# The gate's row sums on VectorE instead of TensorE, in a gated mix of local attention and a token MLP

## The chip, the cores and the metric

The kernel runs on one core of a Trainium2 chip. The metric is the device time of one execution in microseconds (us), as a median of several runs; lower is better. The core has a matmul engine (TensorE, PE in the profile; its weight loads are PEld), a vector engine (VectorE, DVE), a scalar engine for activations (ScalarE, ACT), and GpSimd (POOL). SyncE (SP) issues most DMA transfers; ACT issues some. Each engine works through its own list of instructions in order, and semaphores hold an instruction until what it needs is there.

## What is computed

```python
x = A_x                                               # 1 x 2048 x 512, bfloat16
g = sigmoid((x * gate_w).sum(-1, keepdims=True))      # one gate per row
a = A_ref(x, wqkv, wo)   # attention: 32 heads of 16, each row sees 8 keys, 2 rows apart; then @ wo
b = B_ref(x, w1, b1, w2, b2)
return g * a + (1 - g) * b

def B_ref(x, w1, b1, w2, b2):
    h = layernorm(x)                                  # over the 512 columns
    u = gelu(einsum("bsd,sf->bdf", h, w1) + b1)       # mixes the 2048 rows, F = 1792
    return (einsum("bdf,fs->bds", u, w2) + b2).transpose(0, 2, 1)
```

The gate needs, for each of the 2048 rows, the sum over 512 columns of x times gate_w. The change is about how this sum is formed.

## The kernel before, in words

The 2048 rows are 16 tiles of 128 rows (tile t is `X[:, t, :]`). x is loaded twice: plainly into X, which is normalised in place, and transposed by DMA into XT, which feeds the projections. All buffers are views of one SBUF arena, so a name in the profile is mostly `arena`, and groups are told apart by their line and shape. Many regions are used again: the GELU result UT takes XT's place, the first part of `WQKV` later holds a piece of w2, and `ATX`, which later holds spread attention weights, first serves as two product buffers.

The kernel is written as a list of named operations with their engine, the tokens they read and write and an estimated length. A small planner (`_Sched`) orders each engine's list by these estimates. Where the order matters it is fixed by hand: `chain([...])` makes each named operation follow the one before it (lines 923 to 937). Waits come from the tokens. The order is thus settled when the program is built, and an engine never passes a waiting instruction by.

The steps, by the names used below:

- `pf`, `pj` (line 631, PE): the q, k and v projections; ACT evicts them from PSUM (lines 639, 642).
- `ln1_t` (558, DVE), `ln2`, `ln_rstd`, `ln_nmr`: statistics of tile t and what follows from them; `ln3_t` normalises the tile in place, on ACT (582) or on DVE (586), as `ln3_act` says: tiles 0 to 7 and the even ones of 8 to 15 on ACT, tiles 9, 11, 13 and 15 on DVE.
- `gz` (606, PE): the gate sums as 16 matmuls, with gate_w as a column of weights (GWC) over XT, four at a time in four column groups of the array. `g_tanh` (611, ACT) forms tanh of half the sums as four rows of 512; `d_th0` writes these to DRAM and `d_th1` reads them back as one column per tile (SP). `g_g`, `g_omg`, `g_c2` (619 to 623, DVE) make g, 1 - g and (1 - g) * b2.
- `qkm_h_d_c` (678, DVE): q times k shifted, for the first four (h = 0) and last four (h = 1) keys; `qkr_h_d` (686, PE) sums the products over a head's columns; `lev_h_w` (720, ACT) evicts the logits.
- `msk` (730), `sm_*` (736 to 769, DVE; exp on ACT, 755): masks and softmax over the 8 keys. `d_atx` (ACT's DMA queue): the weights spread to all partitions of a head, in 8 units.
- `avm`, `ava`, `avb`, `avc` (789 to 794, DVE): weights times v, and the sum over keys, unit by unit, two units at a time, into OT. `avc_7` is the last.
- `ph2_ft_qt` (804, PE): the first MLP matmul, 14 blocks of F (ft), each over 16 row tiles in four quarters (qt); `gel_ft` (815, ACT): GELU into UT.
- `ph3a`, `ph3b` (844, PE): the second MLP matmul, two halves for each output tile; `t1_i` (898, ACT): times 1 - g, plus (1 - g) * b2.
- `wo_i` (861, PE): the attention's output projection for tile i; `cmb_i` (873, DVE): g times it plus `t1_i`; `d_out_i` (SP) writes it out through four buffers. `wo_i` uses four PSUM banks in turn, so `wo_4` has to wait for `cmb_0`.

In the DVE chain all `cmb` stand behind `avc_7`. On PE, `wo_0` to `wo_3` stand behind `ph3b_14`, then come `ph3a_15`, `ph3b_15`, `wo_4` and the rest. The planner gives PE the order projections, `gz`, `qkr_1_1`, 44 matmuls of ph2, `qkr_1_3`, the rest of ph2. On SP the chain is:

```python
chain(["d_w2_0", "d_th0", "d_w2_1", "d_th1", "d_w1_4", "d_w2_2", "d_w1_5", "d_w1_6"])
```

Of the kernel before, what the change touches and what calls it, by code (L numbers as in the profile page):

```python
# [5 lines left out]
BF16 = mybir.dt.bfloat16  # L6
# [7 lines left out]
D = 512  # L14
# [274 lines left out]
def _views(nc, es):  # L289
    off = {}  # L290
    cur = [0]

    def region(name, nbytes):
        nbytes = (nbytes + 63) // 64 * 64
        off[name] = cur[0]
        cur[0] += nbytes

    region("X", NST * D * 2)
    region("XT", 4 * S * 2)
    region("WQKV", 4 * 3 * D * 2)  # L300
# [9 lines left out]
    region("BR", 192)  # L310
    region("BT", 192)
    region("IDENT", 128 * 2)
    region("ONES", 128 * 2)
    region("RP", 32 * 2)
    region("SMALL", 2048)
    total = cur[0]
    arena = es.enter_context(nc.sbuf_tensor("arena", [128, total], U8))

    def view(name, dtype, dims, extra=0):
        base = arena[:].bitcast(dtype)  # L320
        pstride = base.ap[0][0]
# [12 lines left out]

def bass_gated_mix__sliding_local_dilated__mixer_token_mlp__prompt_kernel(nc, A_x, A_wqkv, A_wo, B_x, B_w1, B_b1, B_w2, B_b2, gate_w, out, dbg=None):
    with contextlib.ExitStack() as es:
# [43 lines left out]
        THR = view("WQKV", FP32, [(1, SC)])  # L380
        gsc = nc.dram_tensor("gate_rows", (4, 512), FP32)
        so = [0]

        def small(n):
# [12 lines left out]
        TH = small(NST)  # L397
        G = small(NST)
        OMG = small(NST)
        C2 = small(NST)  # L400
        B1C = small(NFT)
        B2C = small(NST)
        BR = view("BR", BF16, [(32, 3), (1, 32)])
        BT = view("BT", BF16, [(32, 3), (1, 32)])
        GWC = BT[:, 2, :]
        assert so[0] * 4 <= 2048

        def col(v_, i):
# [106 lines left out]

        A("pool", lambda e: e.memset(BR, 0.0), 0.2, writes=["br"], name="br0")
        ds_b = sch.dsem("b12")
        for i_, (v_, n_) in enumerate(((B_b1, NFT), (B_b2, NST), (gate_w, 4))):
            vr = v_.rearrange("(t q j) -> q t j", q=4, j=32)
            for q_ in range(4):  # L520
                sch.dma("sp", mk_dma(psub(BR, 32 * q_, n_, 32 * i_, [(1, 32)]), vr[q_]), n_ * 64, ds_b, reads=["br"],
                        writes=["br_%d_%d" % (i_, q_)], deps=throttle(), after=prev_dma(), name="d_b_%d_%d" % (i_, q_), issue=0.45)
        d_w1.append(ld_w1(3))
        A("dve", lambda e: e.transpose(out=BT, in_=BR), 0.2, reads=["br_%d_%d" % (i_, q_) for i_ in range(3) for q_ in range(4)],
          writes=["gwc"], name="t_b")
        A("act", lambda e: e.activation(out=B1C, in_=BT[:, 0, 0:NFT], func=AF.Copy), 0.2, reads=["gwc"], writes=["b1c"], name="b1c")
        A("act", lambda e: e.activation(out=B2C, in_=BT[:, 1, 0:NST], func=AF.Copy), 0.2, reads=["gwc"], writes=["b2c"], name="b2c")
# [65 lines left out]
        def main_bank():  # L593
            b = main_idx[0] % 4
            main_idx[0] += 1
            return b

        def emit_gz():
            bank = main_bank()
            acc = ["acc%d" % bank]  # L600

            def f_gz(e):
                ins = None
                for dt in range(4):
                    for sb in range(4):
                        ins = e.matmul(ps[32 * sb:32 * sb + 32, bank, :], lhsT=sub(GWC, dt, [(0, 32)]), rhs=XT[:, dt, 512 * sb:512 * sb + 512],
                                       start=(dt == 0), stop=(dt == 3), tile_position=(0, 32 * sb))
                return ins

            last_main[0] = A("pe", f_gz, 0.9, reads=ALLXT + ["gwc"], writes=acc, after=[last_main[0]], name="gz")  # L610
            A("act", lambda e: e.activation(out=THR, in_=ps[:, bank, :], func=AF.Tanh, scale=0.5), 1.9, reads=acc,
              writes=["thr", "wqkv0_0"], name="g_tanh", prio=0)
            ds_th = sch.dsem("th")
            sch.dma("sp", mk_dma(gsc.ap(), bass.AP(THR.tensor, THR.offset, [[32 * THR.ap[0][0], 4], [1, 512]])), 8192, ds_th,
                    reads=["thr", "wqkv0_0"], writes=["gsc"], name="d_th0", issue=0.5)
            ds_th2 = sch.dsem("th2")
            sch.dma("sp", lambda e: e.dma_start(TH, gsc.ap().rearrange("b (t p) -> p (b t)", p=128), allow_slow_non_contiguous=True), 8192, ds_th2, reads=["gsc"], writes=["th"],
                    name="d_th1", issue=0.5)
            A("dve", lambda e: e.tensor_scalar(out=G, in0=TH, scalar1=0.5, scalar2=0.5, op0=ALU.mult, op1=ALU.add), 0.15,
              reads=["th"], writes=["g"], name="g_g", prio=0)  # L620
            A("dve", lambda e: e.tensor_scalar(out=OMG, in0=TH, scalar1=-0.5, scalar2=0.5, op0=ALU.mult, op1=ALU.add), 0.15,
              reads=["th"], writes=["omg"], name="g_omg", prio=0)
            A("dve", lambda e: e.tensor_tensor(out=C2, in0=OMG, in1=B2C, op=ALU.mult), 0.15,
              reads=["omg", "b2c"], writes=["c2"], name="g_c2", prio=0)

        def f_proj(tn, dl, sb, bank, d0=0, d1=4, s0=0, s1=512):
            def fn(e):
# [169 lines left out]
        def f_ph2(ft, bank, half):  # L797
# [8 lines left out]
                return ins  # L806
            return fn

        for ft in range(NFT):
            j = ft // 2  # L810
            bank = main_bank()
            for qt in range(4):
                last_main[0] = A("pe", f_ph2(ft, bank, qt), 0.864, reads=["x%d" % t for t in range(4 * qt, 4 * qt + 4)] + ["w1s%d" % (j % 4)],
                                 writes=["acc%d" % bank], after=[last_main[0]], name="ph2_%d_%d" % (ft, qt), prio=0)
# [9 lines left out]
        def ld_w2(j2):  # L824
# [3 lines left out]
            if j2 < 2:  # L828
                dp = [byq["qkr_1_1"]]
            elif j2 == 2:  # L830
                al = ["wqkv%d_%d" % (tn, dt) for tn in range(3) for dt in range(4)]
# [85 lines left out]
        def ln2(hf):  # L917
            return ["ln2%s%d" % (c_, hf) for c_ in "abcd"]

        def lnr(hf):  # L920
# [15 lines left out]
        chain(["ln3_8", "ln3_10", "ln3_12", "ln3_14", "g_tanh", "gel_0", "gel_1"] + ["lev_1_%d" % w for w in range(4)] + ["sm_pre", "sm_exp0", "sm_exp1", "gel_2", "gel_3", "gel_4"] + atn(0) + ["gel_5"] + atn(2) + ["gel_6"] + atn(1) + ["gel_7"] + atn(3)  # L936
              + ["gel_8", "gel_9"] + atn(4) + ["gel_10"] + atn(6) + ["gel_11", "gel_12"] + atn(5) + ["gel_13"] + atn(7) + ["t1_0"])

        if dbg is not None and "keep" in dbg:
            keepf = dbg["keep"]  # L940
# [92 lines left out]
```

## Time and profile before

| | us |
|---|---|
| median of 3 runs | 171.76 (171.66 to 172.13) |
| the profiled execution, whole | 170.96 |
| its span in the profile | 169.2 |
| PE busy in it | 163.5 (97%) |
| DVE busy | 142.8 (84%) |
| ACT busy | 74.4 (44%) |
| POOL busy | 1.0 (1%) |

The profile is one execution, with times from the start of its span. A line of a timeline gives start, length, engine, source line, operation, and output and input with shapes (partitions by elements), then the number of instructions merged into it, and in brackets how long the engine had been idle before and what ended that. Neighbouring instructions of an engine overlap a little in the records, so the length of several is less than the sum of their durations; the "pitch" is the distance from one start to the next. Matmuls are pipelined: one of 512 columns takes 0.379 from start to end, and the next starts 0.216 later.

### The profile page before, as it was taken

The numbers are of one execution on the slowest core, as the hardware profiler recorded it, in microseconds if no ns is written. First come the engines' busy times: TensorE is split into PE (matmuls) and PEld (weight loads), VectorE is DVE, ScalarE is ACT, GpSimd is POOL, SyncE is SP. The second block draws the span as 40 slices with busy tenths as digits, with TensorE's granted clock in tenths as the row PEclk, the third lists the DMA queues.
The fourth block names the chain that finished last, engine by engine and source line by source line (L and its number), as shares of the span: only waits on it lengthen the run. The fifth ranks groups of instructions, "written<-read, shape, count | busy, mean of one in ns | idle before, by whom it ended". The sixth has DMA issues, their size and how long they took to land.

```text
span 169.2 us, 2130 instructions
## 1 busy us (share of the span) xinstructions
PE 163.5 (97%) x850; PEld 76.5 (45%) x865; DVE 142.8 (84%) x122; ACT 74.4 (44%) x112; POOL 1.0 (1%) x9
## 2 busy tenths in 40 slices
PE   7999999999999999999999999999999999999992
PEld 2555555544444444444444444444444444444440
DVE  1009999999999963899999999999999999952874
ACT  0476698898979718691222131131221312211000
POOL 2000000000000000000000000000000000000000
PEclk9999999999999999999999999999999999999999
DMA  5999999939000989973789606472573470002234
GB/s 137 282 299 244 278 326 282 288 105 251 1 0 12 257 175 239 286 188 86 196 222 316 161 16 144 108 200 71 162 217 107 114 217 0 0 27 97 93 128 155
DMA packets 47313, 27.43 MB, mean 162 GB/s; under 512 B 11844, under 2 KB 46148, under 8 KB 47304
## 3 DMA queue, kind: packets, MB, share of 16 engines
q1 hardware_dynamic: 44696, 22.05, 48.6%
q10 hardware_dynamic: 2608, 5.25, 11.9%
q8 instruction: 7, 0.11, 0.3%
q14 instruction: 2, 0.02, 0.0%
HBM read 18.89 MB, written 2.11 MB: 124 GB/s over the span
## 4 chain that ended last, share of the span: by engine, by line
PE 93%; DMA 3%; ACT 2%; issue 1%; DVE 0%
PE ps L844 28%; PE ps L804 28%; PE ps L631 24%; PE ps L861 8%; PE ps L686 3%; DMA arena<-in_A_x_dram 3%; ACT arena L582 1%; DVE arena L873 0%; ACT arena L642 0%
## 5 line engine op out<-in xcount | busy, mean ns | idle before, releaser
L844 PE MATMUL ps<-arena 128*128 128x512 bf16 x220 | 48.5, 379 | 0.2
L804 PE MATMUL ps<-arena 128*128 128x512 bf16 x219 | 48.1, 379 | 0.5 <-ACT arena L582 0.2
L631 PE MATMUL ps<-arena 128*128 128x512 bf16 (+2 forms) x196 | 41.4, 370 | 0.7 <-issue 0.3
L678 DVE TENSOR_TENSOR arena<-arena 128x4096 bf16<-128x4096 bf16 (+1 forms) x12 | 35.6, 2991 | 0.0
L789 DVE TENSOR_TENSOR arena<-arena 128x8192 bf16<-128x8192 bf16 x8 | 35.0, 4419 | 0.0
L804 PEld LDWEIGHTS ps<-arena 128*128 128x128 bf16 x224 | 21.7, 98 | 26.8 <-issue 0.8
L844 PEld LDWEIGHTS ps<-arena 128*128 128x128 bf16 x224 | 21.9, 98 | 26.4
L631 PEld LDWEIGHTS ps<-arena 128*128 128x128 bf16 x200 | 21.9, 113 | 20.5 <-issue 1.0
L898 ACT ACTIVATE arena<-ps,arena 128x512 bf16<-128x512 f32 x16 | 12.5, 778 | 39.4 <-PE ps L844 35.6
L792 DVE TENSOR_TENSOR arena<-arena 128x4096 bf16<-128x4096 bf16 (+1 forms) x16 | 27.0, 1751 | 0.0
L642 ACT ACTIVATE arena<-ps 128x512 bf16<-128x512 f32 x32 | 18.9, 596 | 5.4 <-PE ps L631 5.2
L815 ACT ACTIVATE arena<-ps,arena 128x512 bf16<-128x512 f32 x14 | 9.6, 688 | 24.9 <-PE ps L804 24.7
L558 DVE BATCH_NORM_STATS2 arena<-arena 128x6 f32<-128x512 bf16 x16 | 10.1, 680 | 10.8 <-DMA arena<-in_A_x_dram 10.8
L873 DVE SCALAR_TENSOR_TENSOR arena<-ps,arena 128x512 bf16<-128x512 f32 x16 | 11.7, 749 | 6.7 <-PE ps L861 4.8
L861 PE MATMUL ps<-arena 128*128 128x512 bf16 x62 | 14.0, 379 | 0.1
L639 ACT ACTIVATE arena<-ps 128x512 bf16<-128x512 f32 x16 | 9.0, 596 | 3.8 <-PE ps L631 3.8
L861 PEld LDWEIGHTS ps<-arena 128*128 128x128 bf16 x64 | 6.3, 98 | 7.5
L582 ACT ACTIVATE arena<-arena 128x512 bf16<-128x512 bf16 x12 | 9.2, 803 | 0.0
L736 DVE TENSOR_TENSOR arena<-arena 128x512 bf16<-128x512 bf16 (+4 forms) x11 | 7.3, 667 | 0.8 <-ACT arena L755 0.5
L686 PE MATMUL ps<-arena 128*32 128x512 bf16 x128 | 7.6, 380 | 0.0
L794 DVE TENSOR_TENSOR arena<-arena 128x1024 bf16<-128x1024 bf16 x8 | 5.5, 688 | 0.1
L720 ACT ACTIVATE arena<-ps 128x512 bf16<-128x512 f32 x8 | 4.1, 603 | 2.5 <-PE ps L686 2.5
(42 smaller groups left out, 37.3 us busy)
## 6 DMA issues: line engine op xcount, KB each, us to landing
arena<-in_B_w_dram SPq DMA_DIRECT2D x7, 1024.0 KB, 7.9
arena<-in_B_w_dram SPq DMA_DIRECT2D x8, 896.0 KB, 5.2
arena<-arena ACTq DMA_DIRECT2D x32, 128.0 KB, 2.7
arena<-in_A_x_dram SPq DMA_DIRECT2D x4, 512.0 KB, 5.1
out_dram<-arena SPq DMA_DIRECT2D x16, 128.0 KB, 1.7
arena<-in_A_wqkv_dram ACTq DMA_DIRECT2D x2, 256.0 KB, 2.9
arena<-in_A_wqkv_dram ACTq DMA_DIRECT2D x1, 512.0 KB, 4.3
arena<-in_A_wqkv_dram SPq DMA_DIRECT2D x1, 512.0 KB, 7.1
```

What stands on the lines that cost most here:

```text
L582: A("act", (lambda t_: (lambda e: e.activation(out=X[:, t_, :], in_=X[:, t_, :], func=AF.Identity, scale=col(RSTD, t_), bias=col(NMR, t_)) ...
L631: ins = e.matmul(ps[:, bank, s0:s1], lhsT=lhsT, rhs=XT[:, dt, sb * 512 + s0:sb * 512 + s1], start=(dt == 0 and s0 == 0), stop=(dt == 3))
L642: return lambda e: e.activation(out=dst, in_=ps[:, bank, :], func=AF.Copy)
L678: return lambda e: e.tensor_tensor(out=PBL[buf][:, :, 512 * c0:512 * (c0 + nc_)], in0=in0, in1=in1, op=ALU.mult)
L686: ins = e.matmul(ps[32 * c:32 * c + 32, 4 + wl, :], lhsT=RP, rhs=PBL[buf][:, wl, c * 512:(c + 1) * 512], start=(dl == 0), stop=(dl == 3), ...
L789: A("dve", (lambda o_, i0, i1: (lambda e: e.tensor_tensor(out=o_, in0=i0, in1=i1, op=ALU.mult)))(pv, in0, in1), 4.4, reads=v_res + ["atx_% ...
L792: A("dve", (lambda pv_, n__: (lambda e: e.tensor_tensor(out=pv_[:, 0:n__], in0=pv_[:, 0:n__], in1=pv_[:, n__:2 * n__], op=ALU.add)))(pv, n ...
L804: ins = e.matmul(ps[:, bank, :], lhsT=W1W[:, slot, st, 128 * e_:128 * e_ + 128], rhs=X[:, st, :], start=(st == 0), stop=(st == NST - 1))
L844: ins = e.matmul(ps[:, bank, :], lhsT=W2S[slot][:, ft, 128 * e_:128 * e_ + 128], rhs=UT[:, ft, :], start=(ft == 0), stop=(ft == NFT - 1))
L861: ins = e.matmul(ps[:, WB(i), :], lhsT=OT[:, t, 128 * i:128 * i + 128], rhs=WO[:, t, :], start=(t == 0), stop=(t == 3))
L873: A("dve", (lambda i_: (lambda e: e.scalar_tensor_tensor(out=OUTS[:, i_ % 4, :], in0=ps[:, WB(i_), :], scalar=col(G, i_), in1=T1[:, i_, :] ...
L898: A("act", (lambda i_, bank_: (lambda e: e.activation(out=T1[:, i_, :], in_=ps[:, bank_, :], func=AF.Identity, scale=col(OMG, i_), bias=co ...
```

## The change

The 16 gate matmuls, the tanh over rows and the two DRAM transfers go. x is loaded a second time in its plain layout (tiles 12 to 15 into XB, a quarter of the product buffers in `ATX`; tiles 0 to 11 into XA, over the projection weights once the last projection is done), and gate_w is spread over all partitions (GWB, behind UT). DVE multiplies each tile by GWB and accumulates the sum into a column of GZ (`gz_0` to `gz_15`): six of these before the second masks, ten between the softmax and the first `avm`. `g_tanh` then works on one 128 x 16 tile, between `gel_8` and `gel_9`, and `g_omg`, `g_c2`, `g_g` follow `avm_2`. `ln3` of tiles 8 to 15 all go to ACT. The first three blocks of ph2 run the quarters of tiles 0 to 7 first and those of tiles 8 to 15 after. The load `d_w2_2`, which overwrites XA, goes to the end of its chain and waits for `g_tanh`.

```diff
-        for i_, (v_, n_) in enumerate(((B_b1, NFT), (B_b2, NST), (gate_w, 4))):
+        for i_, (v_, n_) in enumerate(((B_b1, NFT), (B_b2, NST))):
...
-        ln3_act = [t for t in range(NST) if t < 8 or t % 2 == 0]
+        ln3_act = list(range(NST))
...
-        def emit_gz():
-            bank = main_bank()
-            acc = ["acc%d" % bank]
-
-            def f_gz(e):
-                ins = None
-                for dt in range(4):
-                    for sb in range(4):
-                        ins = e.matmul(ps[32 * sb:32 * sb + 32, bank, :], lhsT=sub(GWC, dt, [(0, 32)]), rhs=XT[:, dt, 512 * sb:512 * sb + 512],
-                                       start=(dt == 0), stop=(dt == 3), tile_position=(0, 32 * sb))
-                return ins
...
-            A("act", lambda e: e.activation(out=THR, in_=ps[:, bank, :], func=AF.Tanh, scale=0.5), 1.9, reads=acc,
-              writes=["thr", "wqkv0_0"], name="g_tanh", prio=0)
...
-        emit_gz()
+        GWB = view("XT", BF16, [(1, D)], extra=NFT * D)
+        XA = view("WQKV", BF16, [(D, 12), (1, D)])
+        XB = view("ATX", BF16, [(D, 4), (1, D)], extra=3 * NW * HC)
+        ds_xb = sch.dsem("xb")
+        sch.dma("sp", mk_dma(XB, xv[:, 12:16, :]), 4 * 128 * D * 2, ds_xb, writes=["xb"], name="d_xb")
+        ds_gw = sch.dsem("gw")
+        gsrc = bass.AP(gate_w.tensor, gate_w.offset, [[0, 128], [1, D]])
+        sch.dma("sp", mk_dma(GWB, gsrc), 128 * D * 2, ds_gw, writes=["gwb"], deps=[last_main[0]], name="d_gw")
+        ds_xa = sch.dsem("xa")
+        sch.dma("sp", mk_dma(XA, xv[:, 0:12, :]), 12 * 128 * D * 2, ds_xa,
+                writes=["xa"] + ["wqkv%d_%d" % (tn, dt) for tn in range(3) for dt in range(4)], name="d_xa")
+        for t in range(NST):
+            src = XA[:, t, :] if t < 12 else XB[:, t - 12, :]
+            A("dve", (lambda s_, t_: (lambda e: e.scalar_tensor_tensor(out=s_, in0=s_, scalar=1.0, in1=GWB, op0=ALU.mult, op1=ALU.mult,
+                                                                       accum_out=col(GZ, t_))))(src, t),
+              0.6, reads=["xa" if t < 12 else "xb", "gwb"], writes=["gz%d" % t], name="gz_%d" % t)
+        A("act", lambda e: e.activation(out=TH, in_=GZ, func=AF.Tanh, scale=0.5), 0.25, reads=["gz%d" % t for t in range(NST)],
+          writes=["th"], name="g_tanh", prio=0)
...
+        for ft in range(3):
+            emit_ph2(ft, (0, 1))
         for ft in range(NFT):
...
+            emit_ph2(ft, (2, 3) if ft < 3 else (0, 1, 2, 3))
...
-              + ["ln3_%d" % t for t in range(NST) if t not in ln3_act] + ["qkm_1_2_0", "msk_0", "sm_ma0", "sm_mb0", "qkm_1_3_0",
-                 "msk_1", "sm_ma1", "sm_mb1", "sm_m1", "sm_sub0", "sm_sub1", "g_omg", "g_c2", "g_g"]
-              + ["%s%d" % (n_, h_) for h_ in range(2) for n_ in ("sm_sa", "sm_sb", "sm_s1", "sm_rcp", "sm_nrm")]
+              + ["qkm_1_2_0", "msk_0", "sm_ma0", "sm_mb0", "qkm_1_3_0"] + gz(12, 13, 14, 15, 0, 1) + [
+                 "msk_1", "sm_ma1", "sm_mb1", "sm_m1", "sm_sub0", "sm_sub1"]
+              + ["%s%d" % (n_, h_) for h_ in range(2) for n_ in ("sm_sa", "sm_sb", "sm_s1", "sm_rcp", "sm_nrm")] + gz(*range(2, 12))
...
+        byname["d_xb"].deps.update(byname["qkr_0_3_%d" % w] for w in range(4))
...
-        chain(["d_w2_0", "d_th0", "d_w2_1", "d_th1", "d_w1_4", "d_w2_2", "d_w1_5", "d_w1_6"])
+        chain(["d_xb", "d_gw", "d_xa", "d_w2_0", "d_w2_1", "d_w1_4", "d_w1_5", "d_w1_6", "d_w2_2"])
...
+        chain(["avm_2", "g_omg", "g_c2", "g_g", "ava_0"])
```

More of the change, by code (lines that the diff above doesn't have):

```diff
@@ L309, in _views @@
     region("OUTS", 4 * D * 2)
-    region("BR", 192)
-    region("BT", 192)
+    region("BR", 128)
+    region("BT", 128)
     region("IDENT", 128 * 2)
@@ L379, in bass_gated_mix__sliding_local_dilated__mixer_token_mlp__prompt_kernel @@
         MX = view("OUTS", BF16, [(4 * HC, 2), (2 * HC, 2), (HC, 2), (1, HC)])
-        THR = view("WQKV", FP32, [(1, SC)])
-        gsc = nc.dram_tensor("gate_rows", (4, 512), FP32)
         so = [0]
@@ L399, in bass_gated_mix__sliding_local_dilated__mixer_token_mlp__prompt_kernel @@
         OMG = small(NST)
+        GZ = small(NST)
         C2 = small(NST)
@@ L402, in bass_gated_mix__sliding_local_dilated__mixer_token_mlp__prompt_kernel @@
         B2C = small(NST)
-        BR = view("BR", BF16, [(32, 3), (1, 32)])
-        BT = view("BT", BF16, [(32, 3), (1, 32)])
-        GWC = BT[:, 2, :]
+        BR = view("BR", BF16, [(32, 2), (1, 32)])
+        BT = view("BT", BF16, [(32, 2), (1, 32)])
         assert so[0] * 4 <= 2048
@@ L523, in bass_gated_mix__sliding_local_dilated__mixer_token_mlp__prompt_kernel @@
         d_w1.append(ld_w1(3))
[L524 to L527, printed above, removed]
+        A("dve", lambda e: e.transpose(out=BT, in_=BR), 0.2, reads=["br_%d_%d" % (i_, q_) for i_ in range(2) for q_ in range(4)],
+          writes=["btc"], name="t_b")
+        A("act", lambda e: e.activation(out=B1C, in_=BT[:, 0, 0:NFT], func=AF.Copy), 0.2, reads=["btc"], writes=["b1c"], name="b1c")
+        A("act", lambda e: e.activation(out=B2C, in_=BT[:, 1, 0:NST], func=AF.Copy), 0.2, reads=["btc"], writes=["b2c"], name="b2c")
         WARM = view("OUTS", BF16, [(1, D)], extra=0)
@@ L596, in main_bank @@
             return b
-        def emit_gz():
-            bank = main_bank()
-            acc = ["acc%d" % bank]
-            def f_gz(e):
-                ins = None
-                for dt in range(4):
-                    for sb in range(4):
-                        ins = e.matmul(ps[32 * sb:32 * sb + 32, bank, :], lhsT=sub(GWC, dt, [(0, 32)]), rhs=XT[:, dt, 512 * sb:512 * sb + 512],
-                                       start=(dt == 0), stop=(dt == 3), tile_position=(0, 32 * sb))
-                return ins
-            last_main[0] = A("pe", f_gz, 0.9, reads=ALLXT + ["gwc"], writes=acc, after=[last_main[0]], name="gz")
-            A("act", lambda e: e.activation(out=THR, in_=ps[:, bank, :], func=AF.Tanh, scale=0.5), 1.9, reads=acc,
-              writes=["thr", "wqkv0_0"], name="g_tanh", prio=0)
[L613 to L624, printed above, removed]
         def f_proj(tn, dl, sb, bank, d0=0, d1=4, s0=0, s1=512):
@@ L670, in bass_gated_mix__sliding_local_dilated__mixer_token_mlp__prompt_kernel @@
               writes=["%s5_%d_%d" % (tnames[tn], dl, sb)], name="ev_%s%d_%d" % (tnames[tn], dl, sb), prio=0)
-        emit_gz()
+        GWB = view("XT", BF16, [(1, D)], extra=NFT * D)
[16 more added lines that the diff above has]
+          writes=["th"], name="g_tanh", prio=0)
+        A("dve", lambda e: e.tensor_scalar(out=G, in0=TH, scalar1=0.5, scalar2=0.5, op0=ALU.mult, op1=ALU.add), 0.15,
+          reads=["th"], writes=["g"], name="g_g", prio=0)
+        A("dve", lambda e: e.tensor_scalar(out=OMG, in0=TH, scalar1=-0.5, scalar2=0.5, op0=ALU.mult, op1=ALU.add), 0.15,
+          reads=["th"], writes=["omg"], name="g_omg", prio=0)
+        A("dve", lambda e: e.tensor_tensor(out=C2, in0=OMG, in1=B2C, op=ALU.mult), 0.15,
+          reads=["omg", "b2c"], writes=["c2"], name="g_c2", prio=0)
         def f_qkm(wh, dl, buf, c0, nc_):
@@ L807, in f_ph2, with emit_ph2 @@
             return fn
+        p2bank = {}
+        def emit_ph2(ft, qts):
+            if ft not in p2bank:
+                p2bank[ft] = main_bank()
+            bank = p2bank[ft]
+            j = ft // 2
+            for qt in qts:
+                last_main[0] = A("pe", f_ph2(ft, bank, qt), 0.864, reads=["x%d" % t for t in range(4 * qt, 4 * qt + 4)] + ["w1s%d" % (j % 4)],
+                                 writes=["acc%d" % bank], after=[last_main[0]], name="ph2_%d_%d" % (ft, qt), prio=0)
+        for ft in range(3):
+            emit_ph2(ft, (0, 1))
         for ft in range(NFT):
             j = ft // 2
[L811 to L814, printed above, removed]
+            emit_ph2(ft, (2, 3) if ft < 3 else (0, 1, 2, 3))
+            bank = p2bank[ft]
             A("act", (lambda ft_, bank_: (lambda e: e.activation(out=UT[:, ft_, :], in_=ps[:, bank_, :], func=AF.Gelu_apprx_tanh,
@@ L830, in ld_w2 @@
             elif j2 == 2:
-                al = ["wqkv%d_%d" % (tn, dt) for tn in range(3) for dt in range(4)]
+                al = ["wqkv%d_%d" % (tn, dt) for tn in range(3) for dt in range(4)] + ["gz%d" % t for t in range(12)]
             return sch.dma("sp", mk_dma(W2S[j2 % 3], w2v[:, :, 256 * j2:256 * j2 + 256]), F * 256 * 2, ds,
@@ L918, in ln2, with gz @@
             return ["ln2%s%d" % (c_, hf) for c_ in "abcd"]
+        def gz(*ts):
+            return ["gz_%d" % t for t in ts]
         def lnr(hf):
@@ L925, in bass_gated_mix__sliding_local_dilated__mixer_token_mlp__prompt_kernel @@
               + ["qkm_0_3_2", "qkm_1_0_0"] + ln1(15) + ln2(1) + ["t_b", "qkm_1_1_0"] + lnr(1)
-              + ["ln3_%d" % t for t in range(NST) if t not in ln3_act] + ["qkm_1_2_0", "msk_0", "sm_ma0", "sm_mb0", "qkm_1_3_0",
-                 "msk_1", "sm_ma1", "sm_mb1", "sm_m1", "sm_sub0", "sm_sub1", "g_omg", "g_c2", "g_g"]
-              + ["%s%d" % (n_, h_) for h_ in range(2) for n_ in ("sm_sa", "sm_sb", "sm_s1", "sm_rcp", "sm_nrm")]
+              + ["qkm_1_2_0", "msk_0", "sm_ma0", "sm_mb0", "qkm_1_3_0"] + gz(12, 13, 14, 15, 0, 1) + [
+                 "msk_1", "sm_ma1", "sm_mb1", "sm_m1", "sm_sub0", "sm_sub1"]
+              + ["%s%d" % (n_, h_) for h_ in range(2) for n_ in ("sm_sa", "sm_sb", "sm_s1", "sm_rcp", "sm_nrm")] + gz(*range(2, 12))
               + ["%s_%d" % (n_, u) for k_ in range(4) for n_ in ("avm", "ava", "avb", "avc") for u in USEQ[2 * k_:2 * k_ + 2]] + ["cmb_%d" % i for i in range(NST)])
+        byname["d_xb"].deps.update(byname["qkr_0_3_%d" % w] for w in range(4))
         byname["d_w1_6"].deps.add(byname["d_atx_2_3"])
-        chain(["d_w2_0", "d_th0", "d_w2_1", "d_th1", "d_w1_4", "d_w2_2", "d_w1_5", "d_w1_6"])
+        chain(["d_xb", "d_gw", "d_xa", "d_w2_0", "d_w2_1", "d_w1_4", "d_w1_5", "d_w1_6", "d_w2_2"])
         def atn(u):
             return ["d_atx_%d_%d" % (u, a_) for a_ in range(4)]
+        chain(["avm_2", "g_omg", "g_c2", "g_g", "ava_0"])
         chain(["ph3b_14"] + ["wo_%d" % i for i in range(4)] + ["ph3a_15", "ph3b_15", "wo_4"])
-        chain(["ln3_8", "ln3_10", "ln3_12", "ln3_14", "g_tanh", "gel_0", "gel_1"] + ["lev_1_%d" % w for w in range(4)] + ["sm_pre", "sm_exp0", "sm_exp1", "gel_2", "gel_3", "gel_4"] + atn(0) + ["gel_5"] + atn(2) + ["gel_6"] + atn(1) + ["gel_7"] + atn(3)
-              + ["gel_8", "gel_9"] + atn(4) + ["gel_10"] + atn(6) + ["gel_11", "gel_12"] + atn(5) + ["gel_13"] + atn(7) + ["t1_0"])
+        chain(["ln3_%d" % t for t in range(8, 16)] + ["gel_0", "gel_1"] + ["lev_1_%d" % w for w in range(4)] + ["sm_pre", "sm_exp0", "sm_exp1", "gel_2", "gel_3", "gel_4"] + atn(0) + ["gel_5"] + atn(2) + ["gel_6"] + atn(1) + ["gel_7"] + atn(3)
+              + ["gel_8", "g_tanh", "gel_9"] + atn(4) + ["gel_10"] + atn(6) + ["gel_11", "gel_12"] + atn(5) + ["gel_13"] + atn(7) + ["t1_0"])
         if dbg is not None and "keep" in dbg:
```

## The prediction

> **What bounds the kernel now.** I read the page first, then the chain that ended last, then the timelines of TensorE (PE) and VectorE (DVE).
>
> ```profile
> PE 163.5 (97%) x850; PEld 76.5 (45%) x865; DVE 142.8 (84%) x122; ACT 74.4 (44%) x112; POOL 1.0 (1%) x9
> PE 93%; DMA 3%; ACT 2%; issue 1%; DVE 0%
> ```
>
> PE is never short of work and is 93% of the chain, at a granted clock of 0.998. Whatever leaves PE's queue leaves the span, unless something else becomes late. The only other engine near its limit is DVE, so the second question is where DVE still has room. PE's timeline:
>
> ```profile
> 50.90 1.05 PE L606 MATMUL ps<-arena 128*32 128x512 bf16 x16
> 51.77 1.90 PE L686 MATMUL ps<-arena 128*32 128x512 bf16 x32
> 53.83 9.44 PE L804 MATMUL ps<-arena 128*128 128x512 bf16 x43 [0.16 <-ACT arena L582]
> 63.21 1.91 PE L686 MATMUL ps<-arena 128*32 128x512 bf16 x32
> 152.69 3.18 PE L844 MATMUL ps<-arena 128*128 128x512 bf16 x14
> 155.71 10.52 PE L861 MATMUL ps<-arena 128*128 128x512 bf16 x47
> ```
>
> The columns are start and length in us. L606 is the gate's 16 matmuls; L686 at 51.77 is qkr_1_1 and at 63.21 qkr_1_3; L861 at 155.71 begins with wo_4. DVE's timeline:
>
> ```profile
> 19.32 2.47 DVE L558 BATCH_NORM_STATS2 arena<-arena 128x6 f32<-128x512 bf16 x4
> 50.64 1.38 DVE L586 TENSOR_SCALAR arena<-arena 128x512 bf16<-128x512 bf16 x4
> 57.49 4.42 DVE L678 TENSOR_TENSOR arena<-arena 128x8192 bf16<-128x8192 bf16 x1
> 66.00 0.12 DVE L730 MEMSET arena<- 32x8 bf16 x4 [4.08 <-ACT arena L720]
> 70.08 0.17 DVE L621 TENSOR_SCALAR arena<-arena 128x16 f32<-128x16 f32 x1
> 70.28 0.18 DVE L623 TENSOR_TENSOR arena<-arena 128x16 f32<-128x16 f32 x1
> 70.37 0.17 DVE L619 TENSOR_SCALAR arena<-arena 128x16 f32<-128x16 f32 x1
> 71.00 2.41 DVE L736 TENSOR_TENSOR arena<-arena 128x1024 f32<-128x1024 bf16 x3 [0.46 <-ACT arena L755]
> 80.60 1.23 DVE L769 TENSOR_TENSOR arena<-arena 128x2048 bf16<-128x2048 bf16 x1
> 81.84 8.76 DVE L789 TENSOR_TENSOR arena<-arena 128x8192 bf16<-128x8192 bf16 x2
> 147.21 1.41 DVE L794 TENSOR_TENSOR arena<-arena 128x1024 bf16<-128x1024 bf16 x2
> 150.30 3.34 DVE L873 SCALAR_TENSOR_TENSOR arena<-ps,arena 128x512 bf16<-128x512 f32 x4 [1.68 <-PE ps L861]
> 163.62 3.41 DVE L873 SCALAR_TENSOR_TENSOR arena<-ps,arena 128x512 bf16<-128x512 f32 x5 [0.91 <-DMA out_dram<-arena]
> ```
>
> DVE has two reserves. One is the 4.08 us before the masks (66.00), where it waits for lev_1. The other is at the end. From 81.84 to 148.62 (avc_7 ends) it never rests, then cmb_0 waits 1.68 us for PE. wo_4 writes the PSUM bank that cmb_0 reads, and in the DVE order cmb_0 stands behind avc_7. So if avc_7 slips by several us, wo_4 waits, and PE with it. That is the place where this change is decided.
>
> **What leaves PE.** The 16 gate matmuls run four abreast: 51.77 - 50.90 = 0.87 us, all on the chain. The gain is at most 0.87 us. The gap of 0.16 in front of L804 stays; it stands behind each burst of L686. The ACT part of the gate (tanh with one more table load, 54.44 to 56.33), the two DRAM transfers and the four small gate_w loads lie beside PE and are costed at nothing: ACT waited 2.4 us for PE right after, and SP's next loads are for matmuls over 20 us later.
>
> **The reorder of ph2 and ln3 on ACT.** ACT now normalises tiles 8 to 15, eight instead of four. Four took 2.92 us at 51.50, that is (2.92 - 0.80)/3 = 0.71 each, so eight end at 51.50 + 7 x 0.71 + 0.80 = 57.3. PE first runs the halves of three ft that need tiles 0 to 7 only: 50.90 + 4 x 0.216 + 1.9 (qkr_1_1) + 0.16 + 20 x 0.216 = 58.2 before it needs tile 8, and 59.0 before tile 12. ACT is 1.7 us early, so nothing is lost. qkr_1_3 still stands behind 44 ph2 matmuls, hence 0.87 earlier, and with it lev_1 and the masks: 66.00 - 0.87 = 65.13.
>
> **The new loads.** Before, SP's queue stood from 38 to 53.7 waiting for qkr_1_1, with the DMA engines idle. d_xb (0.5 MB) goes there. d_gw and d_xa (1.57 MB) issue when the last projection is done, 51. The X loads of 0.5 MB took 5.1 us to landing, the w1 loads of 1 MB 7.9. Scaled up to 1.57 MB the latter is 11.9, so d_xa lands between 58 and 63.6. Behind it on SP are d_w2_0 and d_w2_1 (first used at 104) and d_w1_4 (at 83), which can all wait. d_w2_2 now waits for g_tanh, about 87, where before it went at 61; it is used at 116, and its kind takes 5.2 us.
>
> **What DVE gets.** Out go four tensor_scalars: qkm_1_2 moves from 51.94 to 50.53, 1.41 us, so qkm_1_3 ends at 60.50 and frees DVE at 60.42. In come 16 multiply-and-accumulates over 128x512 bf16; no row of before is one. Call the pitch of one p.
> - The product itself: bn_stats (same size and type, also one pass with a sum) runs at (2.47 - 0.68)/3 = 0.60, since neighbours overlap by 0.08. The same opcode from PSUM (L873) runs at (3.41 - 0.75)/4 = 0.665.
> - Writing the sum to a column: the nearest rows are the tiny operations. Four memsets took 0.12 together, 0.07 the first, so under 0.02 more for each; the pair L623, L619 starts 0.09 apart; if the write must wait until the product is drained, it starts after 0.68 and the next waits again, about 0.80 in all (0.68 + 0.03 + 0.09).
> So p lies between 0.61 and 0.80. Below that stands only a faster mode: bf16 tensor_tensor of this size (0.42 long). I take 0.62, with the memsets, as both only write a few values.
>
> [...]
>
> **The sum.** Six products fill the gap: 60.42 + 6 x 0.62 = 64.1, a us before 65.13, costing nothing. If d_xa is late there is that us to spare: gz_0 can start as late as 63.9. The softmax chain is 0.87 earlier, so sm_nrm1 starts at 79.73 and the next instruction 1.15 later (as 75.23 to 76.38), at 80.88. Ten products then stand in front of avm_0, with nothing to hide them: 80.88 + 6.2 = 87.08 instead of 81.84, so +5.24. The three small gate operations, which sat inside the wait for exp (0.46 left of it after them), now lie bare behind avm_2: 0.20 + 0.09 + 0.09 = 0.38. avc_7 ends at 148.62 + 5.24 + 0.38 = 154.24. cmb_0 starts 0.08 sooner and ends at 154.91. A wait across engines cost 0.10 (ln3 ended at 53.73, L804 began at 53.83), so wo_4 can start at 155.01. Undisturbed it would start at 155.71 - 0.87 = 154.84. PE loses 0.17 of its 0.87 us.
>
> Behind wo_4 nothing more is lost: cmb runs at 0.665 and wo at 0.866 a tile, so DVE gains 0.2 us a tile and cmb_4's buffer (written out in 1.7 us) is free in time. ACT's g_tanh between gel_8 and gel_9 waits for gz_11 until 87, when gel_8 is just through.
>
> So the change is -0.87 + 0.17 = -0.70 us. The profiled execution took 170.96 (span 169.2 and 1.76 around it), 0.80 under the median of 171.76; I put the change to the median: 171.06. A change under 0.3% (0.5 us) this kernel's timing can't tell from none.
>
> **The rivals.**
> - *The sum costs some cycles more.* Each 0.01 of p is 0.10 us at wo_4. p of 0.64 to 0.745 gives -0.5 to +0.5 us: no change, about 171.6. For it: the pair of small operations and L873's 0.665. Against: bn_stats, which also ends in a small write, is at 0.60.
> - *The write waits for the drain, DVE becomes the bound: slower.* One mechanism, at wo_4: with p = 0.80 the ten are 8.0 us and the six end at 65.2, 0.1 late; avc_7 ends at 156.1, wo_4 starts 2.1 late, change +1.2: 173.0. It decides above p = 0.69, where the wait at wo_4 eats the whole 0.87. For it: L566 and L569, which depend on their forerunner, start 0.2 after it, not 0.09. Against: those have semaphore waits.
> - *A late transfer.* One output tile took 3.4 us to land instead of 1.7, and cmb waited 0.91. Now, with DVE behind, such a wait close to cmb_4 would reach PE with up to 0.9 us: 172.0. d_xa landing at 65 would cost 1.1: 172.2.
> - *The products run at twice the rate*, p near 0.36: avc_7 is early enough, and the full 0.87 comes: 170.89.
>
> **How the numbers follow.** Forecast (p to 0.64, and the twice-as-fast case): 0.45. Same: 0.22. Drain: 0.25. Late transfer: 0.08, half of it slower, half the same. Faster 0.45, same 0.26, slower 0.29. The range goes from the full gain, 170.85, to p = 0.80 with a bit of late transfer on it, 173.2; the forecast's own is 170.85 to 171.3.
>
> **What would show it.** Right: L606 is gone; the products start 0.62 apart; qkr_1_3 starts at 62.3; DVE's wait before the masks shrinks to 1 us; the first L789 at 87.1; PE's wait in front of wo_4 is 0.1 to 0.3 with cmb as releaser. Wrong: products 0.7 or more apart, a PE wait over 0.9 there, a wait of L804 on ln3, or of DVE on d_xa.

## The result and the profile after

| | before | after |
|---|---|---|
| median of 16 runs, us | 171.56 | 170.81 |
| ratio after to before | | 0.9958 (95%: 0.9945 to 0.997) |
| span of the profiled execution | 169.2 | 168.6 |
| DVE busy | 142.8 | 150.7 |

The change makes the kernel 0.72 us faster (0.0042 x 171.56; 0.5 to 0.9 by the interval; 0.75 by the medians). The forecast was 0.70 faster. The time itself, 170.81, lies 0.04 under the low end of the stated range: the median of before was 171.76 from three runs and is 171.56 from sixteen, which include those three. Ratios here and below leave out slow executions, of which there were two: one of 251.23 us (mean granted clock 0.66) in the first run with ln3 on DVE, and one of before at 173.78.

The page after, engines and the chain that ended last:

```profile
PE 164.0 (97%) x849; PEld 76.1 (45%) x849; DVE 150.7 (89%) x150; ACT 75.4 (45%) x115; POOL 1.0 (1%) x9
...
PE 95%; DMA 3%; DVE 0%; issue 0%
```

DVE works 7.9 us more and is still no part of the chain. PE's timeline after (lines have moved: ph2 is L797, qkr L679, ph3 L847, wo L864):

```profile
50.98 1.03 PE L797 MATMUL ps<-arena 128*128 128x512 bf16 x4
51.93 1.91 PE L679 MATMUL ps<-arena 128*32 128x512 bf16 x32
53.78 8.81 PE L797 MATMUL ps<-arena 128*128 128x512 bf16 x40
62.51 1.91 PE L679 MATMUL ps<-arena 128*32 128x512 bf16 x32
...
151.99 3.19 PE L847 MATMUL ps<-arena 128*128 128x512 bf16 x14
155.03 10.53 PE L864 MATMUL ps<-arena 128*128 128x512 bf16 x48
```

The gate's matmuls are gone and no gap has come in their place. From the start of ph3's last block to wo_4 it is 155.03 - 151.99 = 3.04 us; before it was 155.71 - 152.69 = 3.02. So PE loses 0.02 us at the place where the prediction put 0.17. DVE's timeline after (products L655, masks L723, first avm L782, avc L787, cmb L876):

```profile
60.54 0.68 DVE L655 SCALAR_TENSOR_TENSOR arena<-arena 128x512 bf16<-128x512 bf16 x1
61.15 0.08 DVE L655 DVE_READ_ACCUMULATOR arena<-arena 128x1 f32 x1
61.15 0.69 DVE L655 SCALAR_TENSOR_TENSOR arena<-arena 128x512 bf16<-128x512 bf16 x1
...
65.30 0.13 DVE L723 MEMSET arena<- 32x8 bf16 x4 [1.00 <-ACT arena L713]
81.05 0.69 DVE L655 SCALAR_TENSOR_TENSOR arena<-arena 128x512 bf16<-128x512 bf16 x1
...
87.17 4.42 DVE L782 TENSOR_TENSOR arena<-arena 128x8192 bf16<-128x8192 bf16 x1
...
152.90 1.41 DVE L787 TENSOR_TENSOR arena<-arena 128x1024 bf16<-128x1024 bf16 x2
154.23 12.12 DVE L876 SCALAR_TENSOR_TENSOR arena<-ps,arena 128x512 bf16<-128x512 f32 x16
```

The disputed row is there: writing the sum is an instruction of its own, 0.08 long, but it starts in the same moment as the next product. The products start 0.61 apart: the ten from 81.05 to 87.17 take 6.12. The wait before the masks has shrunk from 4.08 to 1.00. avc_7 ends at 154.31 and the sixteen cmb run on without a rest. wo_4 starts 0.80 after cmb_0 (154.23 to 155.03); the runs with more products, below, show that this is the distance at which PE starts when it has waited for cmb_0.

### The profile page after: what moved, and what is told of

It reads as the page before. It is cut to its first block, busy times and chain, and to the rows that moved or that the text cites. A ratio compares the mean times of both kernels' runs of the same rounds, so it can differ in the third digit from the quotient of the medians.

```text
span 168.6 us, 2142 instructions
## 1 busy us (share of the span) xinstructions
PE 164.0 (97%) x849; PEld 76.1 (45%) x849; DVE 150.7 (89%) x150; ACT 75.4 (45%) x115; POOL 1.0 (1%) x9
## 4 chain that ended last, share of the span: by engine, by line
PE 95%; DMA 3%; DVE 0%; issue 0%
PE ps L797 29%; PE ps L847 29%; PE ps L601 25%; PE ps L864 8%; PE ps L679 4%; DMA arena<-in_A_x_dram 3%; DVE arena L876 0%
## 5 line engine op out<-in xcount | busy, mean ns | idle before, releaser
L797 PE MATMUL ps<-arena 128*128 128x512 bf16 x224 | 48.9, 379 | 0.0
L847 PE MATMUL ps<-arena 128*128 128x512 bf16 x224 | 48.7, 379 | 0.0
L601 PE MATMUL ps<-arena 128*128 128x512 bf16 (+2 forms) x200 | 42.0, 371 | 0.3 <-DMA arena<-in_A_x_dram 0.3
L782 DVE TENSOR_TENSOR arena<-arena 128x8192 bf16<-128x8192 bf16 x8 | 35.0, 4418 | 0.0
L847 PEld LDWEIGHTS ps<-arena 128*128 128x128 bf16 x224 | 21.9, 98 | 26.4
L797 PEld LDWEIGHTS ps<-arena 128*128 128x128 bf16 x224 | 21.7, 98 | 26.8 <-issue 0.8
L612 ACT ACTIVATE arena<-ps 128x512 bf16<-128x512 f32 x32 | 18.9, 596 | 5.4 <-PE ps L601 5.2
L818 ACT ACTIVATE arena<-ps,arena 128x512 bf16<-128x512 f32 x14 | 9.6, 688 | 24.8 <-PE ps L797 24.6
L864 PE MATMUL ps<-arena 128*128 128x512 bf16 x64 | 14.2, 379 | 0.0
L876 DVE SCALAR_TENSOR_TENSOR arena<-ps,arena 128x512 bf16<-128x512 f32 x16 | 11.3, 746 | 0.8
L580 ACT ACTIVATE arena<-arena 128x512 bf16<-128x512 bf16 x16 | 12.0, 802 | 0.0
L609 ACT ACTIVATE arena<-ps 128x512 bf16<-128x512 f32 x16 | 9.0, 597 | 3.8 <-PE ps L601 3.8
L655 DVE SCALAR_TENSOR_TENSOR arena<-arena 128x512 bf16<-128x512 bf16 x16 | 9.9, 686 | 0.0
L864 PEld LDWEIGHTS ps<-arena 128*128 128x128 bf16 x64 | 6.2, 98 | 7.7 <-DVE arena L876 0.3
L679 PE MATMUL ps<-arena 128*32 128x512 bf16 x128 | 7.6, 380 | 0.0
L787 DVE TENSOR_TENSOR arena<-arena 128x1024 bf16<-128x1024 bf16 x8 | 5.5, 688 | 0.1
```

The lines of the kernel that those rows point to most:

```text
L580: A("act", (lambda t_: (lambda e: e.activation(out=X[:, t_, :], in_=X[:, t_, :], func=AF.Identity, scale=col(RSTD, t_), bias=col(NMR, t_)) ...
L601: ins = e.matmul(ps[:, bank, s0:s1], lhsT=lhsT, rhs=XT[:, dt, sb * 512 + s0:sb * 512 + s1], start=(dt == 0 and s0 == 0), stop=(dt == 3))
L612: return lambda e: e.activation(out=dst, in_=ps[:, bank, :], func=AF.Copy)
L679: ins = e.matmul(ps[32 * c:32 * c + 32, 4 + wl, :], lhsT=RP, rhs=PBL[buf][:, wl, c * 512:(c + 1) * 512], start=(dl == 0), stop=(dl == 3), ...
L782: A("dve", (lambda o_, i0, i1: (lambda e: e.tensor_tensor(out=o_, in0=i0, in1=i1, op=ALU.mult)))(pv, in0, in1), 4.4, reads=v_res + ["atx_% ...
L797: ins = e.matmul(ps[:, bank, :], lhsT=W1W[:, slot, st, 128 * e_:128 * e_ + 128], rhs=X[:, st, :], start=(st == 0), stop=(st == NST - 1))
```

## The experiments

The theory (A): the gain is the PE time of the gate's matmuls; everything added on DVE, ACT and the DMA queues is covered, and DVE is exactly early enough at wo_4. Kernels were timed in groups, each with before in it. The changed kernel stands at 0.9958 of before in the result and at 0.9941 in the first group here; where a run belongs to another group, its distance from the changed kernel is given by both ratios, which makes a span of 0.3 us. The interval of the run's own ratio comes on top of it.

### The changed kernel again

> The changed kernel itself, as the reference of this group. Both theories: 0.6 to 0.8 us under the kernel before.

170.58 us against 171.60 for before in the same runs, ratio 0.9941 (0.9918 to 0.9964): 1.0 us under, a little more than expected, with the interval reaching down to 0.6.

### The gate's matmuls put back

```diff
...
+        def f_gx(e):
+            ins = None
+            for dt in range(4):
+                for sb in range(4):
+                    ins = e.matmul(ps[32 * sb:32 * sb + 32, gbank, :], lhsT=RP, rhs=XT[:, dt, 512 * sb:512 * sb + 512],
+                                   start=(dt == 0), stop=(dt == 3), tile_position=(0, 32 * sb))
+            return ins
...
+        last_main[0] = A("pe", f_gx, 0.9, reads=ALLXT + ["rp"], writes=["acc%d" % gbank], after=[last_main[0]], name="gx")
```

> The changed kernel with 16 matmuls of the gate's shape put back in their old place on PE (their result is not used). Theory A, the gain is PE time that left the chain: they cost 0.87 us again, the time equals the kernel before within 0.2 us; the DVE list keeps its times, since the planner puts qkr_1_3 behind 40 ph2 matmuls instead of 44. Rival B, the gain comes from the rest that went with them (tanh with its table load, the trip of the gate through DRAM, the four small loads): the time stays with the changed kernel, within 0.2 us.

171.33, which is 0.75 us over the changed kernel in the same group, and 0.9984 (0.9969 to 1.0) of before. Sixteen matmuls whose result is not used undo most of the gain, so most of the gain is PE time. Rival B, which gave the gain to the tanh, the trip through DRAM and the small loads, expected no loss and falls. By the medians the run stays 0.27 under before, a little more than the 0.2 that A allowed; the interval reaches to no difference, so whether a small rest of the gain has another cause is open. The two traces show none on PE: in both, the 16 matmuls take 0.87 us (here from 50.87 to 51.74), and from the first projection to wo_4 it is 150.29 us (here 155.68 - 5.39, before 155.71 - 5.42). In the changed kernel it is 149.49.

### Ten products left out, or one moved: is DVE already the bound?

```diff
-        for t in range(NST):
+        A("pool", lambda e: e.memset(GZ[:, 2:12], 0.0), 0.2, writes=["gz%d" % t for t in range(2, 12)], name="gz_zero")
+        for t in [0, 1] + list(range(12, 16)):
...
```

The lines behind the dots take gz_2 to gz_11 out of the DVE chain.

> The ten products between the softmax and the first avm left out (ten of sixteen gate columns stay zero). Theory A, DVE was just early enough: avc_7 ends 6.1 us sooner, DVE waits for PE before cmb again, the time stays within 0.2 us of the changed kernel. Rival C, DVE is already the bound at wo_4 and eats part of the gain: 0.2 to 0.4 us faster than the changed kernel.

170.47, 0.11 under the changed kernel, not to be told from it (ratios 0.9937 and 0.9941, each known to 0.002). DVE's timeline without the ten:

```profile
149.73 3.34 DVE L877 SCALAR_TENSOR_TENSOR arena<-ps,arena 128x512 bf16<-128x512 f32 x4 [1.41 <-PE ps L865]
156.21 10.25 DVE L877 SCALAR_TENSOR_TENSOR arena<-ps,arena 128x512 bf16<-128x512 f32 x12 [3.13 <-PE ps L865]
```

Six us of DVE work are gone (avc_7 ends at 148.32), and DVE gives them all back: 1.41 and 3.13 us in waits for PE, and the other 1.5 in cmb that follow PE's pace (0.86 a tile), where the changed kernel has all sixteen in 12.12 us. PE gains next to nothing: from ph3's last block to wo_4 it is 3.02 us here. The second way to give DVE room was to move one product into the us that is left before the masks:

```diff
-  ... gz(12, 13, 14, 15, 0, 1) ...
+  ... gz(12, 13, 14, 15, 0, 1, 2) ...
...
-  ... gz(*range(2, 12))
+  ... gz(*range(3, 12))
```

> A seventh product (gz_2) moved from behind the softmax into the wait before the masks, which had 1.0 us left. Theory A: avc_7 ends 0.6 us sooner, the weight load of wo_4 no longer waits, the time gains 0 to 0.1 us, not to be told from none. Rival C: 0.2 to 0.4 us faster.

170.47 again, ratio 0.9942. The avc end 0.6 us sooner (153.73), and cmb_0 starts at 153.65:

```profile
153.65 12.70 DVE L876 SCALAR_TENSOR_TENSOR arena<-ps,arena 128x512 bf16<-128x512 f32 x16
```

wo_4 starts at 155.04, now 1.39 after cmb_0 and not 0.80, so it no longer waits for it; from ph3's last block (152.02) it is 3.02 us instead of 3.04. The times can't exclude the 0.2 of rival C, the two traces do: what could be won at wo_4 is 0.02 us. This version has 0.6 us of margin there but is not faster.

### More products: where is the edge?

```diff
+        for t in range(2, 2 + n):
+            A("dve", (lambda s_, t_: (lambda e: e.scalar_tensor_tensor(out=s_, in0=s_, scalar=1.0, in1=GWB, op0=ALU.mult, op1=ALU.mult,
+                                                                   accum_out=col(GX, t_ - 2))))(XA[:, t, :], t),
...
```

n stands for the number of the run: 2, 8 or 5. GX is a tile of spare columns; the lines behind the dots put the products behind gz_11 in the DVE chain.

> Two more products behind the ten (into spare columns). Theory A, the edge of what DVE can take lies within 0.2 us of where the change put it: avc_7 ends 1.22 us later, wo_4 starts 1.1 to 1.2 later than in the changed kernel, and the time is 1.1 to 1.2 us longer. Rival E, the four PSUM banks and the faster pace of cmb (0.67 against 0.87 a tile) take up the delay: under 0.4 us longer.

171.61, ratio 1.0012 (0.9994 to 1.0031): 0.9 to 1.2 us over the changed kernel. PE's timeline:

```profile
152.50 3.19 PE L852 MATMUL ps<-arena 128*128 128x512 bf16 x14
156.77 10.53 PE L869 MATMUL ps<-arena 128*128 128x512 bf16 x48 [1.09 <-DVE arena L881]
```

and DVE's first cmb:

```profile
155.97 12.13 DVE L881 SCALAR_TENSOR_TENSOR arena<-ps,arena 128x512 bf16<-128x512 f32 x16
```

The 1.09 in brackets is the idle time after the end of the last matmul. PE would have started the next one 0.16 before that end (0.379 - 0.216), so the time lost is larger, and the distance between starts shows it: 156.77 - 152.50 = 4.27 instead of 3.02, which is 1.25, the two products (1.22) and 0.03. The banks took up nothing: rival E falls. wo_4 starts 0.80 after cmb_0, as in the changed kernel. So the change stands at the very point where DVE becomes the bound, with nothing to spare: every further product counts in full.

> Eight more products behind the ten. Theory A: every one counts in full, 4.9 us on DVE, 4.7 to 4.9 us longer than the changed kernel. Rival E: the part up to 2 us is taken up, so under 3.5 us longer.

177.66, ratio 1.0371: 7.1 to 7.4 us over the changed kernel, where 4.9 were expected. Both theories miss it. The wait at wo_4 is as foreseen; what follows it is not. First PE's timeline:

```profile
151.89 3.19 PE L852 MATMUL ps<-arena 128*128 128x512 bf16 x14
159.83 12.89 PE L869 MATMUL ps<-arena 128*128 128x512 bf16 x48 [4.76 <-DVE arena L881]
```

Then the stretches around it (the columns are stretch, length, busy time and count of PE, PEld, DVE, ACT and POOL, the granted clock, DMA share and GB/s):

```profile
157.20:158.20 1.00, 0.00 (x0) 0.00 (x0) 1.00 (x2) 0.00 (x0) 0.00 (x0) 0.81 0.00 0
158.20:159.20 1.00, 0.00 (x0) 0.00 (x0) 0.96 (x3) 0.00 (x0) 0.00 (x0) 0.50 0.00 0
...
159.80:164.30 4.50, 4.47 (x11) 1.64 (x12) 3.45 (x5) 0.00 (x0) 0.00 (x0) 0.50 0.43 146
164.30:170.00 5.70, 5.70 (x27) 2.53 (x26) 4.45 (x6) 0.00 (x0) 0.00 (x0) 0.97 0.34 115
```

wo_4 starts 159.83 - 151.89 = 7.94 after ph3's last block, 4.92 more than 3.02: eight products (4.90) and 0.02. While PE waits, its granted clock falls to 0.50, and it stays there until some 5 us after work has come back. The 48 matmuls of wo take 12.89 instead of 10.53, so 4.92 + 2.36 = 7.3: the sum holds.

> Five more products behind the ten, between the runs with two (PE waited 1.09 us at wo_4 and the clock stayed at 1.0) and with eight (PE waited 4.76 us and the granted clock was 0.50 for the next 5 us). PE should wait 2.9 us. Theory A, only the wait counts: 2.9 to 3.1 us longer than the changed kernel, clock 1.0 throughout. Rival J, a wait of this length already halves the granted clock afterwards: about 5.3 us longer, wo matmuls 0.63 long behind the wait.

174.74, ratio 1.0187: 3.9 to 4.2 us over the changed kernel, between A's 3.1 and J's 5.3. The four executions fall into two pairs. The profiled one is on theory A's side:

```profile
152.70 3.18 PE L852 MATMUL ps<-arena 128*128 128x512 bf16 x14
158.81 10.53 PE L869 MATMUL ps<-arena 128*128 128x512 bf16 x48 [2.93 <-DVE arena L881]
```

A wait of 2.93 left the clock at 1.0 and wo at 10.53; by the starts 158.81 - 152.70 - 3.02 = 3.09 us were lost, five products (3.06) and 0.03. That execution took 174.32, another 174.05, both with a mean granted clock of 1.0 on record. The other two took 175.16 and 175.21, 0.9 longer, and their mean granted clock is 0.987. As an estimate, that mean over their span of 173.4 is 4.5 us at half clock (0.50, as in the run with eight), more than the 3 us behind the last matmul hold. So in those the clock did fall while there was work; no profile shows where. The same kernel goes either way.

### Without the sum

```diff
...
-  ..., op1=ALU.mult, accum_out=col(GZ, t_)) ...
+  ..., op1=ALU.mult) ...
```

> The sixteen products without the accumulated sum (the gate columns stay zero, so the gate's value is left out). Theory A, writing the sum is nearly free: the products start 0.60 apart instead of 0.61, time unchanged. Rival D, the sum costs a slot of its own that the product's pitch hides by chance: the pitch falls below 0.57.

One execution: 170.54. Ten products on DVE:

```profile
81.32 6.10 DVE L656 SCALAR_TENSOR_TENSOR arena<-arena 128x512 bf16<-128x512 bf16 x10
```

(6.10 - 0.69)/9 = 0.60 apart, against 0.61 with the sum. The sum costs 0.01 us each. Rival D falls.

### ln3 on DVE again

```diff
-        ln3_act = list(range(NST))
+        ln3_act = [t for t in range(NST) if t < 8 or t % 2 == 0]
...
```

The lines behind the dots move the four ln3 from ACT's chain into DVE's, in front of qkm_1_2.

> Tiles 9, 11, 13 and 15 normalised on DVE again, the rest as changed. Theory A: qkm_1_3 ends 1.41 us later, the six products end 0.35 us past the moment at which lev_1 allows the masks, so everything behind is 0.35 later and PE waits that long at wo_4: 0.3 us longer than the changed kernel. Rival F, the move of ln3 to ACT was not needed: no difference (under 0.1).

171.50, ratio 1.0005 (0.9991 to 1.0019): 0.8 to 1.1 us over the changed kernel, three times what A expected, and not F's zero. The trace says why the sum was wrong:

```profile
54.39 9.67 PE L797 MATMUL ps<-arena 128*128 128x512 bf16 x44
```

and DVE's at the masks:

```profile
66.78 0.12 DVE L723 MEMSET arena<- 32x8 bf16 x4 [0.43 <-ACT arena L713]
```

The planner, which settles PE's order by its own estimates, had moved qkr_1_3 behind 4 + 44 ph2 matmuls instead of 4 + 40. That is 0.87 us, the whole of what PE lost at wo_4 in this trace (156.52 - 152.61 - 3.02 = 0.89). DVE, with the four ln3 done, still had 0.43 left before the masks and waited for lev_1. So by this trace the four operations alone would have made the masks 0.87 - 0.43 = 0.44 late, and the later place of qkr_1_3 added the other 0.43. A second run held qkr_1_3 in its place:

```diff
...
+        byname["ph2_2_3"].order.update(byname["qkr_1_3_%d" % w] for w in range(4))
...
```

> Tiles 9, 11, 13 and 15 normalised on DVE as in the earlier run of that edit, but with qkr_1_3 held in the changed kernel's place on PE, behind 44 ph2 matmuls; there the planner had let it slip behind 48, the masks began 1.2 us later although DVE was idle 0.43 us before them, and the time grew by 1.1. Theory A, the 1.1 was the slip of qkr_1_3 (four matmuls, 0.87): with it held only the six products' 0.3 us past the masks' moment is left, PE waits 0.3 to 0.4 at wo_4, 0.3 us longer than the changed kernel. Rival I, the four operations on DVE cost it by themselves: 0.9 to 1.2 us longer.

170.99, ratio 0.9973 (0.9955 to 0.999): 0.3 to 0.5 us over the changed kernel, near A's 0.3; rival I expected 0.9 or more. So about half of the first run's loss was the place of qkr_1_3, the rest the four operations. Its own profile doesn't show this, since it is the longest of its twelve executions (171.85; the shortest took 170.61): PE is idle 0.34 in front of qkr_1_3 for the late qkm_1_3 and 0.63 at wo_4. In it the plain x, for which DVE waits at the start, landed late: bn_stats began at 13.60 instead of 12.68, and DVE ran 0.8 us further behind PE from there on, with no gap before the masks to take it up. Without those 0.8 the masks would be 0.4 late, near A's 0.3.

### ph2 straight through

```diff
-        for ft in range(3):
-            emit_ph2(ft, (0, 1))
...
-            emit_ph2(ft, (2, 3) if ft < 3 else (0, 1, 2, 3))
+            emit_ph2(ft, (0, 1, 2, 3))
```

> The first three blocks of ph2 run straight through tiles 0 to 15 again, ln3 of tiles 8 to 15 stays on ACT. Theory A, the reorder is what hides ln3: the matmuls on tiles 12 to 15 of the first block are reached at 55.5 and ACT is done with tile 15 at 57.4, so PE waits about 1.9 us with ACT line 580 as releaser, and the time is 1.7 to 1.9 us longer than the changed kernel. Rival G, the reorder is worth nothing: no difference (under 0.2).

172.48, ratio 1.0062 (1.0039 to 1.0084): 1.8 to 2.1 us over the changed kernel, and slower than before. PE's timeline:

```profile
53.93 1.90 PE L797 MATMUL ps<-arena 128*128 128x512 bf16 x8
57.61 4.49 PE L797 MATMUL ps<-arena 128*128 128x512 bf16 x20 [1.78 <-ACT arena L580]
```

PE is through with tiles 0 to 11 of the first block at 55.8 and waits 1.78 us for ln3 on ACT. The reorder hides that; rival G falls. Without it the change would have been a loss.

### The second load of x late

```diff
-        chain(["d_xb", "d_gw", "d_xa", "d_w2_0", "d_w2_1", "d_w1_4", "d_w1_5", "d_w1_6", "d_w2_2"])
+        chain(["d_xb", "d_gw", "d_w2_0", "d_w2_1", "d_xa", "d_w1_4", "d_w1_5", "d_w1_6", "d_w2_2"])
```

> d_xa issued behind d_w2_0 and d_w2_1 instead of ahead of them. Theory A, the transfer is hidden only as long as it lands before 63.9: behind 1.8 MB more it lands between 65 and 68, the masks start 1 to 4 us later than 65.3, DVE stays that much late to the end, and the time is 1 to 4 us longer than the changed kernel, equal to the shift of the masks. Rival H, the late load is hidden in any case: no difference (under 0.2).

174.56, ratio 1.0181 (1.0148 to 1.0214): 3.8 to 4.1 us over the changed kernel. DVE's timeline:

```profile
68.41 0.69 DVE L655 SCALAR_TENSOR_TENSOR arena<-arena 128x512 bf16<-128x512 bf16 x1 [4.65 <-DMA arena<-in_A_x_dram]
...
69.67 0.12 DVE L723 MEMSET arena<- 32x8 bf16 x4
```

The load, issued at 55.5, took 12.9 us to land instead of 8.2 from 51.6, gz_0 waited 4.65 us, and the masks came at 69.67 instead of 65.30.

The waits of the same run (who waited for whom, us in total, times, longest):

```profile
PE ps L797 <- ACT arena L818: 2.4, 1, 2.4
...
PE ps L864 <- DVE arena L876: 1.3, 1, 1.3
```

They show a second way to PE that theory A had not named: 1.3 us at wo_4, but 2.4 earlier, in ph2, for GELU (L818), which stands behind the softmax's exp in ACT's list. With 0.16 more for each, as above, 2.6 + 1.5 = 4.1 is the loss.

## Why the prediction was right, and where not

- *What leaves PE, 0.87 us on the chain*: right. Putting the matmuls back cost 0.75 by the medians of one group, 0.87 in its trace.
- *The gap of 0.16 in front of L804 stays*: a misreading, without effect on the sum. The gap is a matmul that the trace of before lacks: it lists 43 of the 44 matmuls there (and 23 of 24 and 35 of 36 behind the earlier bursts), while the weight load of L804 starts at 53.60. After lists all of them, and no gap. So L804 was not waiting for ln3, and the 0.10 for a wait across engines, taken from this place, had no ground. In the runs where wo_4 waits, it starts 0.05 after cmb_0 ends.
- *The pitch p of a product, 0.62 from bn_stats and the memsets*: right, 0.61; the likeness to the memsets was a choice within 0.61 to 0.80, and it came out. The bound of 0.80 (the write waits for the drain) did not come: the write overlaps the next product whole. It is a second instruction in the trace (DVE_READ_ACCUMULATOR, 0.08 long) and costs 0.01: the products start 0.61 apart with it and 0.60 without.
- *The gap before the masks takes six products, 1.0 us left*: right, 1.00. *First avm at 87.1, avc_7's end at 154.24*: 87.17 and 154.31.
- *PE loses 0.17 at wo_4*: the place is right, the amount too much: 0.02 by the distance from ph3's last block. PE and, behind the masks, DVE both ran 0.17 later in this execution than forecast (masks at 65.30, not 65.13), which cancels; the ten products took 6.12 for 6.2, and the hand-over from cmb_0 to wo_4 took 0.05 for 0.10. So that 0.70 came so near to 0.72 is in part luck: with 0.02 in place of 0.17 the same sum gives 0.85, which the interval of 0.5 to 0.9 allows as well.
- *The reorder hides ln3, ACT done at 57.3*: right, 51.67 + 5.74 = 57.41; its worth is 1.8 to 2.1 us.
- *d_xa lands between 58 and 63.6*: right, 51.56 + 8.2 = 59.8. The rival's price of a late landing (1.1 us for 65) was of the right kind: in the run with the late load, 4.65 us of waiting cost 3.8 to 4.1.
- *The range*: wrong, and the step that failed is "I put the change to the median: 171.06", with the low end made of the same anchor less the full gain. Of the 0.25 between 171.06 and 170.81, the anchor is 0.20: the median of three runs stood 0.20 over that of sixteen (171.76 and 171.56), more than a quarter of the change itself, and 0.46 over the median of the other thirteen, 171.30. The change was mis-sized by the other 0.05. The profiled execution, 0.80 lower, had hinted at it. The range allowed for costs of the change upwards and for no error of the anchor downwards; from 171.56 the full gain would have given 170.69. Part of the scatter arises far ahead of the change: in the traces the first 140 projection matmuls, which no run edits, took from 28.67 us to 29.44.

## What to carry to other kernels

Where one engine is 97% busy and another has a reserve, moving work is worth what leaves the full engine, and its price is read at the one place where the other engine hands back its result; here that was a PSUM bank, with nothing to spare: two more products already cost their full 1.2 us, while one product moved into the gap before the masks gives 0.6 of margin at no cost. What makes such a move pay can be the part that looks like housekeeping: here the reorder of three blocks was worth 1.8 to 2.1 us and the place of one load in its queue some 4, against a gain of 0.7. When a change is smaller than the scatter between runs, forecast the difference, and widen the range by what the median of a few runs may be off.

## What the runs showed that was not expected

- DVE_READ_ACCUMULATOR is listed with 0.08 us and costs 0.01: it starts together with the next product.
- A long PE wait near the end cost more than itself. In a wait of 4.76 us the granted clock fell to 0.50, and it came back some 5 us after the work (a mean of 0.50 from 159.80 to 164.30, of 0.97 from there to 170.00), which added 2.36 us; a wait of 2.93 in a profiled execution left it at 1.0. The last matmul had ended at 155.08, and the stretch 157.2 to 158.2 has a mean of 0.81, between 1.00 in the one before and 0.50 in the one behind; as an estimate from these, the clock fell at 157.8, 2.7 us after that end. That is less than the 2.93 that left it at 1.0, so by these two traces the length of the wait alone doesn't decide. The two pairs of executions with five more products, with mean clocks of 1.0 and 0.987, fit that. What decides is not shown.
- A small edit on DVE changed PE's order, since the planner ranks by estimates: qkr_1_3 moved by four matmuls, and that was about half of that run's loss (0.43 of 0.87 by its trace).
